# Where the last rows go: a decode step's gradient kernel, its last half of dK split in two unequal pieces, and y stored from columns

## The chip, the cores and the metric

The kernel runs on one core of one Trainium2 chip. The metric is the device time of one execution in microseconds; the span that the profile gives runs from the core's first to its last instruction and is about 2 us shorter. A core has five compute and control engines here named PE (matrix multiply), DVE (vector), ACT (scalar), POOL (GpSimd) and SP (sync), and sixteen DMA engines that move data between HBM and the on-chip memory of 128 partitions. SP, ACT and POOL each issue transfers; the transfers of one issuer form a queue (in the profile q1 is SP's, q10 is ACT's, q0 is POOL's).

## What is computed

A gated mixture of two branches for one token, forward and backward: the output y and the gradients of nine inputs.

```python
g = sigmoid((x * gate_w).sum(-1))
a = attention(x, k_cache, v_cache, wq, wo)      # 32 heads, 4096 cached keys, head size 128
b = mlp(x, w1, b1, w2)                          # 640 -> 1728 -> 640, h * tanh(softplus(h))
y = g * a + (1 - g) * b                         # out_0, [1, 1, 640], bfloat16
# and the gradients for grad_out:
# out_1 dx, out_2 dK [1, 32, 4096, 128], out_3 dV, out_4 dwq, out_5 dwo,
# out_6 dw1, out_7 db1, out_8 dw2, out_9 dgate_w [640]
```

K, V, dK and dV, 16 transfers of 2 MB each, are most of what is moved.

## The kernel before

The 32 heads are taken in 16 pairs (`i`), four pairs to a group (`g`). For a pair, K and V each come as one transfer of 2 MB: 128 partitions, 16 KB each, into one of seven buffers `kv0` to `kv6`. A pair has 16 slots; PE transposes blocks, makes the scores and the two sums, ACT copies and takes exponentials, DVE makes the outer products of dV and dK over the buffers that held V and K (`outer`, L480), and the full buffer is stored from where it lies (`store_kv`, L755). A store frees the buffer, and `pump` issues the next load. Side work of the MLP and of the projections is planned into the slots by hand.

Pair 15 is written out by hand from L892 on. Its dV and dK are made in quarters by `last_dv` and `last_dk`, and after each second quarter SP stores a half: 128 partitions of 8 KB, 1 MB. In order: the two halves of dV (L900), then the two of dK (L906); between them ACT stores two halves of dwo (L358), and POOL the last of dwq (L514, 640 rows of 1 KB).

At the very end come y, dx and the gradient of `gate_w`. Each stands as 128 partitions by 5 columns in one tile, `fin[:, 0, :]`, `fin[:, 1, :]` and `fin[:, 2, :]`: element 5p + c is in partition p, column c. `fin[:, 0, :]` (y) is written first, at L949; the others need a sum over the partitions on PE (L956) and follow at L959 and L963. PE transposes the three into rows (L967), DVE copies them to `frow`, three partitions of 640 elements (L969), and SP stores each row from one partition in one or two transfers of L976: 640; 636 and 4; 637 and 3 elements. The lengths keep each transfer in one piece on one DMA engine.

Transfers signal their end on semaphores that are taken up in turn: eight for those of SP and ACT together, eight for POOL's. Before a semaphore is used again, the issuing engine waits until the transfer that used it last has landed everywhere. At the end, L1002 in the profile, SP waits for all of these semaphores one after the other, two by two with POOL's; then all engines meet at drains and the program ends.

Of the kernel before, what the change touches and what calls it, by code (L numbers as in the profile page):

```python
# [17 lines left out]
def kernel(  # L18
# [33 lines left out]
    nc = tc.nc  # L52
    P = 128
    _, H, Sk, Dh = A_k_cache.shape
    D = A_x.shape[-1]
# [5 lines left out]
    RC = D // P  # L61
# [16 lines left out]
    dKv = out_2.rearrange("b (i h) (p j) d -> (b i) (h p) (j d)", h=2, j=J)  # L78
# [23 lines left out]
    def C(shape, dt, name):  # L102
        return const.tile(shape, dt, name=name, tag=name)
# [3 lines left out]
    bufs = [big.tile([P, bufw.get(i, KVW)], BF16, name=f"kv{i}", tag=f"kv{i}") for i in range(NBUF)]  # L107
# [369 lines left out]
    def outer(b, col, row, q):  # L477
        n = J // 4
        j0 = q * n
        nc.vector.tensor_tensor(  # L480
            kview(b)[:, j0:j0 + n, :].rearrange("p j (a b) -> p j a b", b=2),
            col[:, j0:j0 + n, :].unsqueeze(2).to_broadcast([P, n, Dh // 2, 2]),
            row.rearrange("p (a b) -> p a b", b=2).unsqueeze(1).to_broadcast([P, n, Dh // 2, 2]),
            ALU.mult)
# [215 lines left out]
    for g in range(NG - 1):  # L700
        i = 4 * g + 4
# [16 lines left out]
    for g in (2, 3):  # L718
        i = 4 * g
# [8 lines left out]
    g, i = NG - 1, NP - 2  # L728
# [163 lines left out]
    i, g = NP - 1, NG - 1  # L892
    q = i % 4
    fb = free_q.popleft()
# [7 lines left out]
    def last_dk(t):  # L902
        outer(fb, st[i]["ds"], Qr[g % 2][:, q, :], t)
        if t % 2:
            h = slice((t - 1) * KVW // 4, (t + 1) * KVW // 4)
            nc.sync.dma_start(dKv[i][:, h], bufs[fb][:, h])  # L906

    for s in range(8):
        slot(i, s)
# [23 lines left out]
    last_dv(2)  # L933
    last_dv(3)
    last_dk(0)
    last_dk(1)
    for rc in range(RC):
        dx_sum(g, NG + g, CB, GC, rc)
        dwq_row(g, CB, GC, rc)
    st_dwq(g * GC + CA, (g + 1) * GC, nc.gpsimd)  # L940
    last_dk(2)
    last_dk(3)

    fin = C([P, 3, RC], BF16, "fin")
# [2 lines left out]
    gb = C([P, RC], F32, "gb")  # L947
    nc.vector.tensor_scalar(gb[:], b_acc[:], omg[:], None, ALU.mult)
    nc.vector.tensor_tensor(fin[:, 0, :], ga[:], gb[:], ALU.add)  # L949
    amb = C([P, RC], F32, "amb")  # L950
    nc.vector.tensor_tensor(amb[:], a_acc[:], b_acc[:], ALU.subtract)
    dgp = C([P, 1], F32, "dgp")
# [14 lines left out]
        nc.tensor.transpose(fr_ps[:, c, :], fin[:, :, c], idb[:])  # L967
    frow = C([3, P, RC], BF16, "frow")
    nc.vector.tensor_copy(frow[:].rearrange("r p c -> r c p"), fr_ps[:])  # L969
    flat = frow[:].rearrange("r p c -> r (p c)")  # L970
    for r, (n, v) in enumerate(((5, out_0.rearrange("a b n -> (a b) n")), (6, out_1.rearrange("a b n -> (a b) n")),
                                (7, out_9.rearrange("(a n) -> a n", a=1)))):
        m = D // n * n
        for c0, c1, k in ((0, m, n), (m, D, 1)):
            if c1 > c0:
                nc.sync.dma_start(v[:, c0:c1].rearrange("a (n x) -> a n x", n=k),  # L976
                                  flat[r:r + 1, c0:c1].rearrange("a (n x) -> a n x", n=k))

# [1 line left out]
_INS = ['A_x', 'A_k_cache', 'A_v_cache', 'A_wq', 'A_wo', 'B_x', 'B_w1', 'B_b1', 'B_w2', 'gate_w', 'grad_out']  # L980
# [26 lines left out]
```

## Time and profile before

| | us |
|---|---|
| median of 3 runs | 404.56 (403.58 to 404.89) |
| profiled execution, its time | 404.45 |
| profiled execution, its span | 402.3 |
| DVE done with `fin[:, 0, :]` | 386.7 |
| SP's issue of the last half of dK | 386.3 |
| DVE done with `frow` | 391.6 |
| SP's issues of the small stores | 391.6 to 396.5 |

Times inside the execution are from the start of its span. The DMA engines moved 164.71 MB in 15867 packets, 409 GB/s on the mean: half of it reading HBM, half of it writing. PE, DVE and ACT are busy for 76, 73 and 66% of the span, POOL for 6%. A packet in the page's sense is one run of bytes moved by one DMA engine; a semaphore's update by a DMA engine is a packet of 4 bytes. A landing is the moment at which the update of a semaphore is recorded.

### The profile page before, as it was taken

How to read it: one execution, taken by the hardware profiler on the slowest of the kernel's cores; microseconds unless marked ns; L12 is line 12 of the kernel's file. 1: busy time of each engine (PE TensorE's matmuls, PEld its weight loads, DVE VectorE, ACT ScalarE, POOL GpSimd, SP SyncE). 2: the span in 40 equal slices, each digit the busy share in tenths (PEclk: the TensorE clock that was granted, in tenths of full speed). 3: DMA queues.
4: the chain of work that ended last, by engine and by line, in shares of the span. 5: the costliest groups of instructions: out<-in, count | busy, mean ns of one | idle time of the engine just before them, and what ended most of it. 6: DMA issues, size and time to landing. Idle time of an engine off the chain costs nothing.

```text
span 402.3 us, 10310 instructions
## 1 busy us (share of the span) xinstructions
PE 303.7 (76%) x4242; PEld 249.0 (62%) x4249; DVE 293.4 (73%) x650; ACT 264.2 (66%) x539; POOL 23.6 (6%) x47
## 2 busy tenths in 40 slices
PE   3879977987778675978889969845789898887410
PEld 3567866866567564866678748725568676675200
DVE  3759677789876595979887948751895697788770
ACT  3547453677567867787766668843377998876730
POOL 3000100001000010100001000000000000000000
PEclk9989998999899699999999989988699899999655
DMA  8999999999999999999999999999999999999992
GB/s 274 428 408 428 427 422 423 428 418 389 414 425 426 420 368 427 422 427 429 433 428 423 430 423 435 423 427 427 428 424 433 424 418 425 421 426 428 402 413 83
DMA packets 15867, 164.71 MB, mean 409 GB/s; under 512 B 1624, under 2 KB 1819, under 8 KB 6092
## 3 DMA queue, kind: packets, MB, share of 16 engines
q1 hardware_dynamic: 8842, 94.08, 55.8%
q0 software_dynamic: 5376, 63.42, 37.5%
q10 hardware_dynamic: 1602, 6.56, 4.3%
q8 instruction: 33, 0.54, 0.5%
q14 instruction: 14, 0.11, 0.1%
HBM read 82.03 MB, written 82.03 MB: 408 GB/s over the span
## 4 chain that ended last, share of the span: by engine, by line
DMA 31%; issue 20%; PE 18%; DVE 17%; ACT 9%; POOL 1%; SPq 1%; ACTq 0%; POOLq 0%; DVEq 0%
DMA wq<-in_A_wq_dram 10%; DVE kv L480 9%; PE tr L374 7%; DMA out_dram<-kv 6%; DMA wo<-in_A_wo_dram 6%; DMA wq<-in_B_w_dram 6%; DMA kv<-in_A_k_cache_dram 4%; ACT tch L377 3%; PE tr L448 2%; PE S L384 2%; DVE junk L290 1%; ACT p_dup L424 1%; PE dq L434 1%; PE a_ps L340 1%; ACT tch L443 1%
## 5 line engine op out<-in xcount | busy, mean ns | idle before, releaser
L377 ACT COPY tch<-tr 128x512 f32<-128x512 f32 x256 | 145.1, 587 | 65.3 <-PE tr L374 60.1
L374 PE MATMUL tr<-idf,kv 128*128 128x128 f32 x1024 | 171.6, 294 | 21.1 <-DMA kv<-in_A_v_cache_dram 10.5
L374 PEld LDWEIGHTS tr<-idf,kv 128*128 128x128 f32 x1024 | 119.7, 150 | 49.3 <-issue 32.4
L384 PEld LDWEIGHTS <-tch 128*128 128x128 bf16 x2048 | 89.7, 98 | 21.6 <-ACT tch L377 15.4
L480 DVE TENSOR_TENSOR kv<-p_dup,Dr 128x2048 bf16<-128x2048 bf16 x64 | 76.8, 1220 | 19.7 <-ACT p_dup L424 19.4
L480 DVE TENSOR_TENSOR kv<-ds_dup,Qr 128x2048 bf16<-128x2048 bf16 x64 | 76.8, 1220 | 0.4
L384 PE MATMUL dP<-dR,tch 128*128 128x48 bf16 x1024 | 47.1, 185 | 10.5 <-ACT tch L377 10.3
L384 PE MATMUL S<-qR,tch 128*128 128x48 bf16 x1024 | 47.7, 186 | 1.1 <-ACT tch L377 0.5
L290 DVE SCALAR_TENSOR_TENSOR junk<-wo,da_bc 128x640 bf16<-128x640 bf16 x32 | 26.3, 822 | 13.8 <-DMA wo<-in_A_wo_dram 13.1
L448 PE MATMUL tr<-idf,tch 128*128 128x128 f32 x128 | 22.0, 297 | 18.2 <-ACT tch L443 18.0
L757 POOL DMA_DIRECT2D out_dram<-kv x25 | 13.4, 536 | 297.1 <-DVE kv L480 251.9
L448 PEld LDWEIGHTS tr<-idf,tch 128*128 128x128 f32 x128 | 14.0, 145 | 20.8 <-ACT tch L443 19.8
L352 ACT ACTIVATE wq<-dqrow,xf 128x1024 bf16<-128x1024 bf16 (+2 forms) x30 | 25.1, 860 | 2.6 <-DVE wq L507 2.3
L507 DVE SCALAR_TENSOR_TENSOR wq<-wq,dqrow 128x1024 bf16<-128x1024 bf16 (+2 forms) x30 | 25.1, 863 | 0.2
L434 PE MATMUL o<-kv,e_m 128*32 128x512 bf16 x256 | 20.4, 400 | 0.0
L434 PE MATMUL dq<-kv,ds_m 128*32 128x512 bf16 x256 | 19.5, 384 | 0.9 <-DVE ds_m L470 0.9
L424 ACT ACTIVATE p_dup<-e_m,rz 64x128 bf16<-64x128 bf16 x32 | 12.7, 397 | 7.7 <-DVE rz L418 7.3
L352 ACT ACTIVATE wo<-da_bc,o8f 128x640 bf16<-128x640 bf16 x20 | 15.9, 825 | 1.3 <-PE a_ps L340 0.8
L411 ACT ACTIVATE e_m<-S,negM 64x64 bf16<-64x64 f32 x32 | 10.5, 329 | 6.3 <-DVE negM L406 5.7
L281 ACT CAST Qr<-q_ps 64x256 bf16<-64x256 f32 x16 | 5.9, 367 | 12.3 <-PE q_ps L277 12.2
L474 ACT COPY ds_dup<-ds_m 64x128 bf16<-64x128 bf16 x32 | 9.5, 296 | 6.4 <-DVE ds_m L470 5.8
L602 DVE SCALAR_TENSOR_TENSOR junk<-wq,db_bc 128x640 bf16<-128x640 bf16 (+1 forms) x14 | 11.5, 820 | 1.9 <-ACT db_bc L256 1.7
(169 smaller groups left out, 279.2 us busy)
## 6 DMA issues: line engine op xcount, KB each, us to landing
out_dram<-kv POOLq DMA_DIRECT2D x25, 2048.0 KB, 16.7
kv<-in_A_v_cache_dram SPq DMA_DIRECT2D x16, 2048.0 KB, 24.0
kv<-in_A_k_cache_dram SPq DMA_DIRECT2D x15, 2048.0 KB, 20.3
out_dram<-kv SPq DMA_DIRECT2D x5, 2048.0 KB, 29.3
wo<-in_A_wo_dram SPq DMA_DIRECT2D x4, 1280.0 KB, 42.9
out_dram<-kv SPq DMA_DIRECT2D x4, 1024.0 KB, 15.5
out_dram<-wo POOLq DMA_DIRECT2D x3, 1280.0 KB, 23.5
wq<-in_A_wq_dram SPq DMA_DIRECT2D x2, 1280.0 KB
```

The costliest lines, as they stand in the source:

```text
L290: nc.vector.scalar_tensor_tensor(junk[:], in0=wob[g % 2][:, k, :], scalar=1.0, in1=da_bc[:], op0=ALU.mult, op1=ALU.mult, accum_out=do8[g % ...
L352: nc.scalar.mul(dst, src, col)
L374: nc.tensor.transpose(tp[:, t, :], src[:, 4 * c + t, :], idf[:])
L377: nc.scalar.copy(dst[:].rearrange("p a b e -> p (a b e)").bitcast(F32), tp[:].rearrange("p a b -> p (a b)"))
L384: nc.tensor.matmul(ps[:, 4 * B:4 * B + W].rearrange("p (a b) -> p a b", b=4), lhsT=src[:, t, :, e], rhs=col[:, e, :, :].rearrange("p a b - ...
L424: nc.scalar.activation(p[HS[hh]], e_m[i % 2][HS[hh], 0:J, hh].unsqueeze(2).to_broadcast([64, J, 2]), ACT.Copy, scale=st[i]["rz"][HS[hh], h ...
L434: nc.tensor.matmul(st[i][key][c:c + 32].rearrange("p a b -> p (a b)"), lhsT=cols[:, 4 * g:4 * g + 16, :].rearrange("p a b -> p (a b)"), rh ...
L448: nc.tensor.transpose(tp[:, 126 * t:126 * t + P], st[i][key + "r"][:, t, :], idf[:])
L480: nc.vector.tensor_tensor(kview(b)[:, j0:j0 + n, :].rearrange("p j (a b) -> p j a b", b=2), col[:, j0:j0 + n, :].unsqueeze(2).to_broadcast ...
L507: nc.vector.scalar_tensor_tensor(w, in0=w, scalar=1.0, in1=dqrow[g % 2][:, c0:c1], op0=ALU.mult, op1=ALU.mult, accum_out=dq_acc[:, rc, par ...
L602: nc.vector.scalar_tensor_tensor(junk[0:n, :], in0=w2row(k), scalar=1.0, in1=db_bc[0:n, :], op0=ALU.mult, op1=ALU.mult, accum_out=dact[0:n ...
L757: eng.dma_start(dst, bufs[b][:, 0:J * Dh])
```

## The change

The last half of dK is stored in two transfers: first partitions 76 to 127 (52 rows), then partitions 0 to 75 (76 rows). 52 is thirteen times four, 76 is four times nineteen; the pieces are meant to run over thirteen DMA engines and over the first four. y is stored by SP directly from `fin[:, 0, :]`, five elements of 2 bytes from each partition, in four transfers of 5, 6, 7 and 110 partitions, placed in the program right after L949. The other two rows still go by way of `frow`, now in one transfer each, issued by POOL; these are cut into sixteen pieces of 40 elements in the built program. The transposes and the copy to `frow` stay as they were, the y row among them.

```diff
@@ last_dk
         if t % 2:
             h = slice((t - 1) * KVW // 4, (t + 1) * KVW // 4)
-            nc.sync.dma_start(dKv[i][:, h], bufs[fb][:, h])
+            for p0, p1 in (((76, P), (0, 76)) if t == 3 else ((0, P),)):
+                nc.sync.dma_start(dKv[i][p0:p1, h], bufs[fb][p0:p1, h])
...
     nc.vector.tensor_tensor(fin[:, 0, :], ga[:], gb[:], ALU.add)
+    y_v = out_0.rearrange("a b (p c) -> (a b p) c", c=RC)
+    for p0, p1 in ((0, 5), (5, 11), (11, 18), (18, P)):
+        nc.sync.dma_start(y_v[p0:p1], fin[p0:p1, 0, :])
...
     nc.vector.tensor_copy(frow[:].rearrange("r p c -> r c p"), fr_ps[:])
-    flat = frow[:].rearrange("r p c -> r (p c)")
-    for r, (n, v) in enumerate(((5, out_0.rearrange("a b n -> (a b) n")), (6, out_1.rearrange("a b n -> (a b) n")),
-                                (7, out_9.rearrange("(a n) -> a n", a=1)))):
-        m = D // n * n
-        for c0, c1, k in ((0, m, n), (m, D, 1)):
-            if c1 > c0:
-                nc.sync.dma_start(v[:, c0:c1].rearrange("a (n x) -> a n x", n=k),
-                                  flat[r:r + 1, c0:c1].rearrange("a (n x) -> a n x", n=k))
+    for r, v in ((1, out_1.rearrange("a b n -> (a b) n")), (2, out_9.rearrange("(a n) -> a n", a=1))):
+        nc.gpsimd.dma_start(v, frow[r:r + 1].rearrange("r p c -> r (p c)"))
```

In SP's order the second piece of the half takes a semaphore of its own, so each small store that follows uses the semaphore after the one that it had.

## The prediction

> **What bounds the kernel now.** I read the page's slices first, then busy time by stretches at the end, then the transfers inside the last stretches, and last what SP waits for. On the page DMA stands at nine tenths in nearly every slice and drops only in the last one: the kernel is bound by its transfers, and the end is theirs too. The stretches of the end (columns: us, busy time of PE, PEld, DVE, ACT and POOL with counts, granted clock, DMA share, GB/s):
>
> ```profile
> 390.00:392.00 2.00, 0.00 (x0) 0.00 (x0) 1.55 (x1) 0.00 (x0) 0.00 (x0) 0.50 1.01 417
> 392.00:394.00 2.00, 0.00 (x0) 0.00 (x0) 0.00 (x0) 0.00 (x0) 0.00 (x0) 0.50 0.87 340
> 394.00:396.00 2.00, 0.00 (x0) 0.00 (x0) 0.00 (x0) 0.00 (x0) 0.00 (x0) 0.50 0.15 59
> 396.00:398.00 2.00, 0.00 (x0) 0.00 (x0) 0.00 (x0) 0.00 (x0) 0.00 (x0) 0.50 0.06 25
> 398.00:400.00 2.00, 0.00 (x0) 0.00 (x0) 0.00 (x0) 0.00 (x0) 0.00 (x0) 0.50 0.07 29
> ```
>
> The compute engines are done at 391.6. From 396 on, 0.06 of sixteen DMA engines are busy: one engine works alone at some 26 GB/s. How the other fifteen end is in finer stretches:
>
> ```profile
> 393.20:393.60 0.40, 0.00 (x0) 0.00 (x0) 0.00 (x0) 0.00 (x0) 0.00 (x0) 0.50 0.93 362
> 393.60:394.00 0.40, 0.00 (x0) 0.00 (x0) 0.00 (x0) 0.00 (x0) 0.00 (x0) 0.50 0.47 188
> 394.00:394.40 0.40, 0.00 (x0) 0.00 (x0) 0.00 (x0) 0.00 (x0) 0.00 (x0) 0.50 0.38 154
> 394.40:394.60 0.20, 0.00 (x0) 0.00 (x0) 0.00 (x0) 0.00 (x0) 0.00 (x0) 0.50 0.21 82
> 394.60:395.90 1.30, 0.00 (x0) 0.00 (x0) 0.00 (x0) 0.00 (x0) 0.00 (x0) 0.50 0.06 25
> ```
>
> A share times 16 is the number of engines busy: 15, then 7.5, 6 and 3.4, and 1 after 394.6. So fifteen engines end between 393.5 and 394.6, on average at 393.9 (their busy time after 393.2, 10.7 us, over 15). The sixteenth, the laggard, ends at 400.54. What it moves last, between 398.08 and 400.54, and in the 2.14 us before:
>
> ```profile
> DMA packets 9, 0.07 MB, mean 27 GB/s; under 512 B 1, under 2 KB 1, under 8 KB 1
> ...
> DMA packets 11, 0.05 MB, mean 24 GB/s; under 512 B 4, under 2 KB 5, under 8 KB 5
> ```
>
> The first line is eight rows of 8 KB and one 4-byte semaphore write: the laggard's share, 8 of 128 rows, of the second half of dK (L906, issued at 386.28). Eight rows take 2.45 us, **0.306 us a row**. Before them come the rows of the first half, whose semaphore write is at 398.08. SP then waits for exactly this landing:
>
> ```profile
> SPq L1002 <- DMA out_dram<-kv: 4.4, 1, 4.4
> ...
> SPq L976 <- DMA out_dram<-kv: 2.7, 1, 2.7
> ```
>
> The semaphore events put the landings on the laggard at 391.29 and 395.93 (two halves of dV), 398.51 and 400.95 (two halves of dK). SP passes 0.02 us after the last and walks through eight more waits, 0.06 us each, to the drains; the span ends at 402.29, so 1.34 us after the landing. If the last landing is one that SP asks for five waits later, only 1.01 us follow.
>
> **The change, part by part.** *dK's last half.* One transfer of 8 rows on each of 16 engines becomes 52 rows over thirteen engines (4 each) and 76 rows over the first four (19 each). In rows: engines 13 to 15 lose 8, engines 4 to 12 lose 4, engines 0 to 3 have 23 in place of 8, so 15 more. At 0.306 us: -2.45, -1.22 and +4.59 us. No row of this trace shows a transfer split over 13 or 4 engines; the price of a row on a busy engine is bounded by the laggard's 0.306 alone and by 0.309 for the time of one packet, which is the same. The second issue costs SP another 0.33 us (the row of L906's issues) at 386.6, hidden by backlog: the fifteen other engines land the first half of dK only between 387.7 and 390.5. It uses a semaphore whose last transfer landed at 381.47, so it waits for nothing.
>
> Engines 0 to 3 now end at 393.5 to 394.6 plus 4.59: 398.1 to 399.2. Of fifteen ends that average 393.9 the latest of four lies near 394.4, so I take 399.0. The laggard ends at 398.09 if it is one of the last three, at 399.32 if it is one of the nine in the middle.
>
> *y in columns.* Four transfers of 5, 6, 7 and 110 rows of 10 bytes read fin, which DVE has at 386.72, in place of the transposed row at 391.56. SP takes up semaphores in turn, and each next use waits for the transfer that used it before: by the order of the changed program the piece of 5 waits for the store of dK of the step before (laggard, 387.22), the piece of 6 for the first half of dV (391.29), the piece of 7 for the second (395.93), the 110 go out right behind, at about 396.5. Behind SP's stall stand only these and the end. So y is not earlier, but it is in time: the small stores before took 1.06 us from issue to landing (396.21 to 397.28), which would be 397.6. On the first four engines, though, the 110 rows stand behind the 76; they land after these, at about 399.05 + 0.41 (the laggard's last row took 0.41 us from its end to its landing) = 399.45. Their packets cost little: the first loads move eight 10-byte rows in 0.015 us. This transfer is the one that SP asks for five waits later. The five old stores on SP (4.88 us from first to last, 2.7 of it the wait shown) go; they landed by 397.28 and were worth nothing.
>
> *dx and dgw on POOL.* Two stores of sixteen 80-byte pieces are issued after 391.56; POOL's issues took 0.54 us (L757) to 0.82 us (L514), so both are out by 393.3. On the laggard they stand behind POOL's last store, which ends there at 395.94, and land near 396.5. POOL's drain ended 1.69 us after its last landing (396.38 to 398.07), so now at about 398.2: cover of over a microsecond. Without that cover each microsecond would be one of time. DVE and PE get no new wait.
>
> **The sum.** The two groups race. If the laggard is one of the last three, the end is that of the first four: 399.45 + 1.01 = 400.46, so 1.83 us less. If it is one of the nine: 399.32 + 0.41 = 399.73, and 1.01 to 1.34 on top: 400.74 to 401.07, so 1.2 to 1.55 less. The profiled execution took 404.45 with a span of 402.29; it stands 0.11 under the median of 404.56. From that median: 402.7, or 403.0 to 403.35. What I forecast is **402.8**, the first case leaning to the second. The ends of the first case are 398.1 and 399.2 for the first four, so 399.56 to 400.66 of span, 401.8 to 402.9.
>
> The Trainium skill ("DMA: Bandwidth & Descriptors", section "Latency and other measured facts") calls DMA engines 7 and 15 the usual slow ones. No run here names the laggard's number; 15 would give the 402.7 above and 7 the 403.0.
>
> **The rivals.** *The laggard is among the first four: slower.* Then its last half costs 15 rows more, +4.59 us, less the 0.33 for the order of waits: 404.56 + 4.26 = 408.8. It decides from the place of one engine. For it: any engine but one is possible. Against: the 1280-byte stores of L976 are each one packet on one engine, and that engine had its rows done by 394, so at least one of the low places is not the laggard's. By counting the fifteen left, 3 in 15; I give 0.13, as the next rival takes some too.
>
> *The first four become the bound altogether.* It is the same price of 4.59 us against the laggard's lead, 400.54 - 394.6 = 5.9 us at least. The change pays only while that lead exceeds 4.6 less the 0.33. Here it does by 1.7 us; an execution with a lead of 4 us would be 0.3 us slower. The semaphore events show the lead as it grows: 0.3 to 0.5 us around 140, 4.2 at 299, 6.5 at 376, 6.6 at the end; steady at the end, and the three times lie within 1.3 us. This is inside the forecast's spread, with 0.05 on the slower side.
>
> The Trainium skill (same page, section "Rules for kernel authors") speaks against such splits: two transfers to disjoint partitions share the same engines, so one transfer of 128 partitions is better. That holds for engines that end together; the rows above show one that ends 6 us late. With even ends it would make the last half 4.59 us dearer.
>
> *The split does not fall as it says.* If both pieces spread evenly over all sixteen engines, the laggard keeps about 8 rows and lands at 400.95; what is left is the 0 to 0.33 us of the order of waits: 404.2 to 404.6. For it: no transfer of 13 or 4 engines is in this trace. Against: a row of 1280 bytes did go to one engine alone. I give 0.10.
>
> **How the numbers follow.** Forecast case 0.77, laggard in the first four 0.13, no split 0.10. About 0.3% (1.2 us) is what a measurement of this kernel can tell from no change. In the forecast case the gain is 1.2 to 1.85 us with a spread of half a microsecond between executions: 0.58 faster, 0.14 within, 0.05 slower. The split rival gives 0.02 faster, 0.07 within, 0.01 slower; the laggard rival 0.13 slower. Together 0.60, 0.21, 0.19. The range runs from 401.6 (ends of the first four at their earliest, and 0.2 of noise) to 404.6 (no split), and leaves out the laggard rival and 0.05 of tails.
>
> **What would show it.** In the changed profile: after about 394.6 four or five engines are busy (a share of 0.25 to 0.3) until near 398, with the rate at 100 to 130 GB/s; the last landing near 399.5, and the span near 400.5. A share of 0.06 to the end with a span over 402 means that nothing moved; one engine alone to past 404 means that the laggard is one of the four. POOL's drain past 399 would mean that dx and dgw have become the end. A piece of 110 that is issued after 397 breaks the reading of SP's waits.

## The result, and the profile after

| | before | after |
|---|---|---|
| median, same chip and session | 404.37 (403.05 to 406.31) | 406.61 (404.43 to 408.62) |
| ratio | | 1.0053, interval 1.0037 to 1.0070 |
| profiled execution, its time | 404.45 | 408.19 |
| profiled execution, its span | 402.3 | 406.0 |

The kernel became slower, by 2.2 us; 1.8 us less had been forecast, and 406.61 lies above the range. The profiled execution stands 1.6 above its own median: it issues the last half of dK at 387.90, against 386.28 before. That lag arose near 200 us, far ahead of anything the change touches (the 57th of the 128 outer products of `outer` began at 202.9, against 200.5), and another execution of the same program, experiment e1, had that one at 199.9. So 1.6 us of what follows is taken off as drift.

The stretches of the end, of the changed kernel, with the columns of the prediction's first fence (the 16 DMA engines' share and GB/s last):

```profile
394.00:396.00 2.00, 0.00 (x0) 0.00 (x0) 0.00 (x0) 0.00 (x0) 0.52 (x2) 0.50 0.55 206
396.00:398.00 2.00, 0.00 (x0) 0.00 (x0) 0.00 (x0) 0.00 (x0) 0.00 (x0) 0.50 0.36 138
398.00:400.00 2.00, 0.00 (x0) 0.00 (x0) 0.00 (x0) 0.00 (x0) 0.00 (x0) 0.50 0.37 78
400.00:402.00 2.00, 0.00 (x0) 0.00 (x0) 0.00 (x0) 0.00 (x0) 0.00 (x0) 0.50 0.22 82
402.00:404.00 2.00, 0.00 (x0) 0.00 (x0) 0.00 (x0) 0.00 (x0) 0.00 (x0) 0.50 0.04 13
```

The split does what it says: after 396 five engines and more are busy (0.36 times 16), not one. But between 398 and 400 the same share moves 78 GB/s in place of 138: the engines are occupied and deliver little. What the changed kernel moved from 397.3 to 398.9, and from 398.9 to 400.5:

```profile
DMA packets 105, 0.21 MB, mean 131 GB/s; under 512 B 79, under 2 KB 79, under 8 KB 80
...
DMA packets 15, 0.07 MB, mean 46 GB/s; under 512 B 6, under 2 KB 6, under 8 KB 6
```

79 packets in the first stretch are small: 60 of them are ten-byte pieces of y, all between 397.5 and 398.2. They are gone by 398.9, and in the 1.6 us behind them only nine rows get through. Single rows of 8 KB took up to 1.57 us here, where the price was 0.306. SP's waits for landings of stores from `kv`, at the end and at the store of y:

```profile
SPq L1000 <- DMA out_dram<-kv: 3.4, 2, 2.6
SPq L953 <- DMA out_dram<-kv: 3.4, 2, 3.0
```

By the semaphore events the 76 rows land at 402.42, 402.73, 402.79 and 404.29, the last 1.5 us after the last row's end (402.82). Then the four pieces of y land one behind the other, at 404.47, 404.64, 404.82 and 405.00. SP passes its last waits 0.17 to 0.18 us apart in place of 0.06, and is done at 405.2.

### The profile page after: what moved, and what is told of

It is laid out like the page before. It is cut to its first block, busy times and chain, and to the rows that moved or that the text cites. A ratio compares the mean times of both kernels' runs of the same rounds, so it can differ in the third digit from the quotient of the medians.

```text
span 406.0 us, 10320 instructions
## 1 busy us (share of the span) xinstructions
PE 309.6 (76%) x4249; PEld 252.6 (62%) x4249; DVE 293.5 (72%) x650; ACT 264.1 (65%) x539; POOL 24.6 (6%) x49
## 4 chain that ended last, share of the span: by engine, by line
issue 28%; DMA 26%; DVE 17%; PE 14%; ACT 9%; POOL 1%; SPq 1%; POOLq 0%; ACTq 0%; DVEq 0%
DMA out_dram<-kv 11%; DVE kv L480 9%; DMA wo<-in_A_wo_dram 6%; DMA kv<-in_A_k_cache_dram 6%; PE tr L374 5%; DMA kv<-in_A_v_cache_dram 4%; ACT tch L377 3%; DVE junk L290 3%; PE tr L448 2%; PE S L384 1%; PE a_ps L340 1%; ACT tch L443 1%; PE dq L434 1%; ACT p_dup L424 1%; DVE wq L507 1%
## 5 line engine op out<-in xcount | busy, mean ns | idle before, releaser
L374 PE MATMUL tr<-idf,kv 128*128 128x128 f32 x1024 | 173.4, 296 | 18.4 <-DMA kv<-in_A_k_cache_dram 9.5
L374 PEld LDWEIGHTS tr<-idf,kv 128*128 128x128 f32 x1024 | 121.5, 152 | 46.9 <-issue 31.9
L384 PEld LDWEIGHTS <-tch 128*128 128x128 bf16 x2048 | 91.0, 99 | 22.6 <-ACT tch L377 16.1
L384 PE MATMUL S<-qR,tch 128*128 128x48 bf16 x1024 | 48.7, 188 | 1.1 <-ACT tch L377 0.5
```

The costliest lines, as they stand in the source:

```text
L374: nc.tensor.transpose(tp[:, t, :], src[:, 4 * c + t, :], idf[:])
L384: nc.tensor.matmul(ps[:, 4 * B:4 * B + W].rearrange("p (a b) -> p a b", b=4), lhsT=src[:, t, :, e], rhs=col[:, e, :, :].rearrange("p a b - ...
```

## The experiments

Each kernel ran beside the kernel before on the same chip. Theory A puts the loss on the split: rows piled on four engines cost more there than the laggard's price. Theory B puts it on y's ten-byte stores. Runs e1 to e4, e5 to e8 and e9 to e11 are one session each (before: 404.52, 404.68 and 404.89), each session on another chip.

**The changed kernel again (e1), no edit.**

> The changed kernel unaltered, for a second profile and for times beside those of the runs that follow. Theory A (the pile): the 19 rows on each of the first four engines set the end, and they cost more than the 0.306 us a row of the prediction, because engines that end together hold each other up, as five of them did from 398.9 to 400.5 in the profile after (46 GB/s where 131 went before). Theory B (the small stores): the 10-byte stores behind the rows land one after the other, 0.17 us each, and POOL's two stores hold its drain to 404.5; the rows alone would be a gain of 1.2 to 1.8 us, as forecast. Theory C (one execution): the stall is chance and the profiled one was unlucky. Expected by A and B: 406.0 to 407.0 median, 1.6 to 2.4 us over the kernel before, the last landing of the 76 rows at 402.5 or later; by A the rate in the last 5 us before the last row falls under 100 GB/s again; by C there is no such fall, and the span is under 404.5.

405.53, ratio 1.0020 [1.0003, 1.0037]: slower again, by 1.0 us, and 1.1 under the first session's median; 406.0 to 407.0 had been expected. The two intervals just touch at their ends: the change costs 2.2 us in one session and 1.0 in the other. Times below are compared with the kernel before in the same session. Its end, in stretches:

```profile
397.10:398.10 1.00, 0.00 (x0) 0.00 (x0) 0.00 (x0) 0.00 (x0) 0.00 (x0) 0.50 0.35 132
398.10:399.10 1.00, 0.00 (x0) 0.00 (x0) 0.00 (x0) 0.00 (x0) 0.00 (x0) 0.50 0.14 42
399.10:401.40 2.30, 0.00 (x0) 0.00 (x0) 0.00 (x0) 0.00 (x0) 0.00 (x0) 0.50 0.00 0
```

Here the rows end at 398.93 and the last packet at 399.04. That is as early as the prediction had it, but only because this execution issues the half at 385.32, 1.0 us earlier than before. Then nothing moves for 2.3 us: the share is 0.00. The landings of dK come until 401.43, the last ones of y's four pieces from 401.62 to 402.18. The fall of the rate that theory A asked for isn't there, and the span of 403.2 is under the 404.5 of theory C (a chance stall in the first profile); but the time is lost here too. In one execution it goes in long packets, in the other between the last packet and its landing; a price per packet sees neither.

**The split alone (e2).** Old small stores, dK in two pieces:

```diff
-            nc.sync.dma_start(dKv[i][:, h], bufs[fb][:, h])
+            for p0, p1 in (((76, P), (0, 76)) if t == 3 else ((0, P),)):
+                nc.sync.dma_start(dKv[i][p0:p1, h], bufs[fb][p0:p1, h])
```

> The kernel before with the last half of dK as 52 and 76 rows; the small stores as before, from rows, by SP. Theory A (the pile): slower than before by 1.3 to 2.3 us, with the four engines ending at 401 or later by the profile. Theory B (the small stores): faster than before by 1 to 1.8 us, the last landing near 399.5 to 400, as the prediction had it.

404.14, ratio 0.9991 [0.9977, 1.0005]: neither figure. The split alone does not slow the kernel, so A's loss of 1.3 to 2.3 us isn't there; the full gain of B does not come either. Its end in stretches, and its longest wait at the end:

```profile
394.60:396.60 2.00, 0.00 (x0) 0.00 (x0) 0.00 (x0) 0.00 (x0) 0.00 (x0) 0.50 0.31 125
396.60:398.60 2.00, 0.00 (x0) 0.00 (x0) 0.00 (x0) 0.00 (x0) 0.00 (x0) 0.50 0.31 127
398.60:400.60 2.00, 0.00 (x0) 0.00 (x0) 0.00 (x0) 0.00 (x0) 0.00 (x0) 0.50 0.14 59
```
```profile
SPq L1003 <- DMA out_dram<-kv: 1.3, 2, 0.9
```

Five engines at a share of 0.31 and 125 GB/s: this is the picture the prediction drew, and the rows follow one another at 0.306 us on each. On the first four engines they end at 399.34, 399.45, 399.88 and 399.93. The 76 rows land at 400.27 at the latest, the 52 on the laggard at 399.82. But the last of the five small stores is issued only at 398.6 and stands on the first engine behind the pile; SP's last waits then go from 400.28 to 401.17, 0.89 us where five of 0.06 had been. Some 0.6 us of the gain is spent there.

Another part is lost ahead of all this. In the kernel before, the stretch from 390 to 392 has a share of 1.01 and 417 GB/s (the first line of the prediction's first fence). The same stretch here (first line) and in e9 (second line), which has the same split and no column store either:

```profile
390.00:392.00 2.00, 0.00 (x0) 0.00 (x0) 1.56 (x1) 0.00 (x0) 0.00 (x0) 0.50 0.98 263
390.00:392.00 2.00, 0.04 (x1) 0.00 (x0) 1.91 (x1) 0.00 (x0) 0.00 (x0) 0.50 0.96 230
```

The engines are nearly as occupied as before and deliver 63 and 55% of it. 19 of the 31 rows begun in this stretch of e2 took more than 0.35 us, the longest 1.20; before, none of 82 did. All seven kernels with the last half in two pieces show it (230 to 330 GB/s), and none of the six with the half in one (380 to 427). From 388 to 394 the rows of e2 took 10.9 us more than at 0.309 each, some 0.7 us for each of sixteen engines if it falls on them evenly (an estimate). So rows are also stretched without any ten-byte write, by the split itself; what in it does so, no run separates.

**The small stores alone (e3).** The changed kernel with dK whole:

```diff
-            for p0, p1 in (((76, P), (0, 76)) if t == 3 else ((0, P),)):
-                nc.sync.dma_start(dKv[i][p0:p1, h], bufs[fb][p0:p1, h])
+            nc.sync.dma_start(dKv[i][:, h], bufs[fb][:, h])
```

> The kernel before with the last half of dK whole, and y stored from columns by SP in pieces of 5, 6, 7 and 110, dx and the gradient of gate_w by POOL, as in the changed kernel. Theory A (the pile): within 0.6 us of before, up to 0.7 slower from the small stores' landings in a row behind the laggard's last rows. Theory B (the small stores): slower by 1.5 us or more, with POOL's drain or the 110 rows of y as the last to end.

406.37, ratio 1.0043 [1.0028, 1.0058]: 1.85 us slower with no split at all. Its stretches around the piece of 110 partitions, then its transfers from 398.23 to 400.315 and from 400.325 to 402.49:

```profile
397.20:398.20 1.00, 0.00 (x0) 0.00 (x0) 0.00 (x0) 0.00 (x0) 0.00 (x0) 0.50 0.11 26
398.20:400.30 2.10, 0.00 (x0) 0.00 (x0) 0.00 (x0) 0.00 (x0) 0.00 (x0) 0.50 0.06 12
400.30:402.40 2.10, 0.00 (x0) 0.00 (x0) 0.00 (x0) 0.00 (x0) 0.00 (x0) 0.50 0.07 27
```
```profile
DMA packets 6, 0.02 MB, mean 12 GB/s; under 512 B 3, under 2 KB 3, under 8 KB 3
...
DMA packets 9, 0.07 MB, mean 30 GB/s; under 512 B 1, under 2 KB 1, under 8 KB 1
```

Of the rows, only the laggard's are left, and most of the loss can be read off this one engine: from 398.2 to 400.3 its rate is 12 GB/s, before and after 26 and 27. Three rows took 0.65, 0.63 and 0.80 us in place of 0.31, 1.14 us lost; the next eight went at 0.306 again. That is where 100 of the 110 ten-byte writes, whose packets ran from 397.2 to 397.6, land on ten other engines (397.97 to 399.77). At the end the landings follow one another from 403.21 to 403.96, and from the first of them to the end of the span it is 1.83 us, 0.48 more than before. Together that makes 1.6 of the 1.85 us. All four pieces of y land late on the laggard, the piece of five too, so the laggard is one of the first five engines.

**A pile on the first four, nothing else (e4).** 4 and 124 rows; 124 is four times 31, so all 128 rows go to the first four, 32 each:

```diff
-            nc.sync.dma_start(dKv[i][:, h], bufs[fb][:, h])
+            for p0, p1 in (((124, P), (0, 124)) if t == 3 else ((0, P),)):
+                nc.sync.dma_start(dKv[i][p0:p1, h], bufs[fb][p0:p1, h])
```

> The kernel before with the last half of dK as 4 and 124 rows, both of a number of rows that puts them on the first four engines: 32 rows on each of the four, none on the other twelve; small stores as before. It measures the price of a row on the four: against 52 and 76 rows (23 on each of the four) nine rows more. Prediction's price (0.306 us a row, no collisions): the four end 24 rows, 7.3 us, later than in the kernel before, at about 401.7, so 1.2 us slower than before and 2.8 slower than the kernel with 52 and 76 rows alone. Theory A (the pile costs more than that): 4 to 6 us slower than before. Theory B says the same as the prediction's price.

406.70, ratio 1.0075 [1.0046, 1.0103], 2.2 us slower by the medians, where 1.2 had been expected by the price; three of the twelve times lie at 410.4 to 410.9 and lift the ratio. Its end in stretches:

```profile
396.00:398.00 2.00, 0.00 (x0) 0.00 (x0) 0.00 (x0) 0.00 (x0) 0.00 (x0) 0.50 0.31 131
...
398.40:400.00 1.60, 0.00 (x0) 0.00 (x0) 0.00 (x0) 0.00 (x0) 0.00 (x0) 0.50 0.24 102
400.00:401.80 1.80, 0.00 (x0) 0.00 (x0) 0.00 (x0) 0.00 (x0) 0.00 (x0) 0.50 0.25 102
```

Five engines until 398.12, when the laggard ends by itself; then four, at 102 GB/s, 25 each. Nothing is dear about the pile once only four engines are left: rows that follow one another begin 0.306 us apart here too. Against e2 each of the four has nine rows more, and the latest ends at 402.88 against 399.93, 2.95 us; by the price it would be 2.75. The laggard is not among the first four; with e3 it is the fifth. The miss over the 1.2 us is the base: 402.88 less 24 rows (32 less the 8 they had before) of 0.306 is 395.5, not 394.4.

**y in columns, alone (e5).** dK whole; dx and dgw as rows by SP, one transfer each:

```diff
+    for p0, p1 in ((0, 5), (5, 11), (11, 18), (18, P)):
+        nc.sync.dma_start(y_v[p0:p1], fin[p0:p1, 0, :])
...
-    for r, (n, v) in enumerate(((5, out_0...), (6, out_1...), (7, out_9...))):
+    for r, n, v in ((1, 5, out_1...), (2, 5, out_9...)):
```

> The kernel before with y alone stored from columns by SP (5, 6, 7 and 110 partitions, ten bytes each, right after L949); the last half of dK whole; dx and the gradient of gate_w by SP from rows, one transfer each. Theory B1 (ten-byte writes): the hundred-odd ten-byte writes take 1 to 2.5 us to land, and rows that other engines write meanwhile, the laggard's among them, take 0.6 to 0.8 us in place of 0.31; with four landings in a row behind the laggard's last (0.18 us each in place of 0.06) that makes 1.2 to 1.9 us over the kernel before. Theory B2 (POOL): the two stores that moved to POOL are the cost, by what they put on the laggard's queue and by POOL's drain; y from columns then costs under 0.5 us.

406.25, ratio 1.0041 [1.0023, 1.0059]: the loss of e3 without POOL's part. Transfers in its windows 394.91 to 396.75, 396.75 to 398.45 and 398.44 to 400.28:

```profile
DMA packets 119, 0.05 MB, mean 28 GB/s; under 512 B 112, under 2 KB 113, under 8 KB 113
...
DMA packets 4, 0.02 MB, mean 14 GB/s; under 512 B 1, under 2 KB 1, under 8 KB 1
...
DMA packets 9, 0.06 MB, mean 32 GB/s; under 512 B 1, under 2 KB 2, under 8 KB 2
```

112 small packets go by in the first window with the laggard at its usual rate. In the second, behind them, it gets three packets over 8 KB through in 1.7 us: two rows took 0.635 and 1.056 us, 1.07 lost. In the third window it is back at the usual rate. The same print as in e3, at another time and on one engine alone. The profiled execution is the fastest of eight (404.98): it issues the half at 385.21, 1.07 us earlier than before, which in this one execution makes up for the rows.

**dx and dgw on POOL, alone (e6).** dK whole, y as a row by SP:

```diff
-    for r, (n, v) in enumerate(((5, out_0...), (6, out_1...), (7, out_9...))):
+    for r, n, v in ((0, 5, out_0...),):
...
+    for r, v in ((1, out_1...), (2, out_9...)):
+        nc.gpsimd.dma_start(v, frow[r:r + 1].rearrange("r p c -> r (p c)"))
```

> The kernel before with dx and the gradient of gate_w alone on POOL (sixteen pieces of 80 bytes each); y by SP from its row as before, the last half of dK whole. Theory B1 (ten-byte writes): within 0.5 us of before, POOL's drain ending over a microsecond ahead of SP. Theory B2 (POOL): slower by 1.2 us or more.

404.50, ratio 0.9990 [0.9972, 1.0008]: nothing. Thirty-two pieces of 80 bytes, stored by POOL, hold up no row. With e5 the parts add up roughly: +1.6 and -0.2, against +1.85 in e3, which is of another session.

**y eight microseconds earlier (e7).** `fin[:, 0, :]` is made right behind the sum it needs and stored in one transfer of 128 partitions at 380.70, when all engines are still loaded:

```diff
     a_cols(g)
+    ...
+    nc.vector.tensor_tensor(fin[:, 0, :], ga[:], gb[:], ALU.add)
+    y_v = out_0.rearrange("a b (p c) -> (a b p) c", c=RC)
+    nc.sync.dma_start(y_v, fin[:, 0, :])
```

> The kernel before with y made right after a_acc, some 8 us earlier than before, and stored at once from columns by SP in one transfer of 128 partitions; dx and the gradient of gate_w by SP from rows, one transfer each. Nothing of y is left behind the last rows. Theory B1 in its strong form (ten-byte writes hold up all rows wherever they fall): slower than before by 0.8 to 1.5 us, since the laggard is busy then too. In its weak form (only what stands on the path at the end costs): within 0.5 us of before. Theory B2: within 0.5 us.

405.42, ratio 1.0029 [1.0010, 1.0047]: 0.7 us by the medians, between the two bands expected, and not free there either. Its stretches around most of the ten-byte packets (381.5 to 382.4):

```profile
381.50:382.50 1.00, 0.00 (x0) 0.00 (x0) 1.00 (x2) 1.00 (x2) 0.00 (x0) 0.50 0.49 173
382.50:383.50 1.00, 0.00 (x0) 0.00 (x0) 1.00 (x2) 0.55 (x2) 0.00 (x0) 0.50 0.35 57
383.50:384.50 1.00, 0.00 (x0) 0.00 (x0) 1.00 (x2) 1.00 (x2) 0.00 (x0) 0.50 0.91 329
```

57 GB/s at a share of 0.35, and three of the five rows begun in that microsecond took 1.01 to 1.33 us. But a share of 0.35 also says that engines lacked queued work, and three small operations of DVE (0.55 us) came forward with y. How the 0.7 us divides between these is open; only the long rows are the print of e3 and e5.

**60 and 68 rows, the three rows by POOL (e8).** 60 is fifteen times four, 68 four times seventeen; y joins dx and dgw on POOL:

```diff
-            for p0, p1 in (((76, P), (0, 76)) if t == 3 else ((0, P),)):
+            for p0, p1 in (((68, P), (0, 68)) if t == 3 else ((0, P),)):
...
-    for p0, p1 in ((0, 5), (5, 11), (11, 18), (18, P)):
-        nc.sync.dma_start(y_v[p0:p1], fin[p0:p1, 0, :])
...
-    for r, v in ((1, out_1...), (2, out_9...)):
+    for r, v in ((0, out_0...), (1, out_1...), (2, out_9...)):
```

> A candidate for a better version: the last half of dK as 60 rows (fifteen engines, 4 each) and 68 (the first four, 17 each), and y, dx and the gradient of gate_w all from rows by POOL, so that SP has nothing behind the rows. Against the kernel with 52 and 76 rows alone (0.4 us faster than before) the first four have two rows less (0.6 us) and the landings behind them, 0.9 us in that profile, shrink to the waits' 0.3. Theory B1: 0.8 to 1.5 us faster than before. Theory B2: no faster than before, as POOL's three stores and its drain end last.

405.45, ratio 1.0022 [1.0004, 1.0041]: a miss. The drains at its end:

```profile
L998 POOLq DRAIN  x3: 40/93/8694, 393.7 to 402.9; - x3
L998 SPq DRAIN  x3: 7/7/7, 401.7 to 402.7; - x3
```

POOL's first drain starts at 393.7 and takes 8.69 us, to 402.4; SP stands ready at 401.7. So POOL sets the end, by 0.7 us. Its pieces on the first four engines wait among their many rows, the last lands at 400.61, and the drain ends 1.8 us after that.

**The changed kernel with y as a row (e9).** The split and POOL's stores of dx and dgw stay; only y goes back to one transfer from `frow`, by SP:

```diff
-    for p0, p1 in ((0, 5), (5, 11), (11, 18), (18, P)):
-        nc.sync.dma_start(y_v[p0:p1], fin[p0:p1, 0, :])
...
+    nc.sync.dma_start(out_0..., flat[0:1]...)
```

> The changed kernel with one part undone: y goes by SP from its row, in one transfer on one engine, as before the change; the 52 and 76 rows and POOL's two stores stay. Theory B1 (ten-byte writes are the cost): 1.2 to 2.2 us faster than the changed kernel, so 0 to 1 us faster than before, like the kernel with the split alone. If the split and the rest were the cost (theory A): within 0.5 us of the changed kernel, 1 us or more slower than before.

403.50, ratio 0.9963 [0.9949, 0.9978]: 1.4 us faster than before, more than the 0 to 1 expected. The one edit against the changed kernel turns the sign. Its end in stretches:

```profile
395.60:396.60 1.00, 0.00 (x0) 0.00 (x0) 0.00 (x0) 0.00 (x0) 0.00 (x0) 0.50 0.31 127
...
397.60:398.60 1.00, 0.00 (x0) 0.00 (x0) 0.00 (x0) 0.00 (x0) 0.00 (x0) 0.50 0.32 131
398.60:399.60 1.00, 0.00 (x0) 0.00 (x0) 0.00 (x0) 0.00 (x0) 0.00 (x0) 0.50 0.29 123
399.60:400.60 1.00, 0.00 (x0) 0.00 (x0) 0.00 (x0) 0.00 (x0) 0.00 (x0) 0.50 0.04 18
```

Five engines at 123 to 131 GB/s with no gap up to 399.6: the stretch that broke down to 78 in the changed kernel is whole. The first four end between 399.24 and 400.39, the 76 rows land at 400.71, 0.3 us behind, and SP is done at 401.16. POOL's drain ends at 401.1, level with it.

**Two rows in columns (e10).** dK whole; y and dx each in two transfers of 18 and 110 partitions:

```diff
+    for p0, p1 in ((0, 18), (18, P)):
+        nc.sync.dma_start(y_v[p0:p1], fin[p0:p1, 0, :])
...
+    for p0, p1 in ((18, P), (0, 18)):
+        nc.sync.dma_start(x1_v[p0:p1], fin[p0:p1, 1, :])
```

> The kernel before with two outputs from columns in place of one: y in pieces of 18 and 110 partitions, and dx likewise, all by SP; the gradient of gate_w from its row; the last half of dK whole. The dose is doubled: 256 ten-byte writes in place of 128. Theory B1: each hundred or so of these writes costs the laggard about 1.1 us in slowed rows, twice 1.1, and landings in a row behind its last rows up to 0.4: 2 to 3 us slower than before, against 1.6 with y alone from columns. If it is the number of landings at the end and not the writes (theory B3): 1.6 us or less, as with y alone.

407.08, ratio 1.0051 [1.0032, 1.0071], 2.2 us: in the band expected if ten-byte writes hold rows up. In its trace four rows begun between 394.2 and 396.5 took 0.60 to 0.94 us, 1.7 us more than at 0.309, against 1.07 in e5. But the interval overlaps that of e5 (one column store, 1.0041), so that a second one adds its full price is not shown.

**60 and 68 rows, the three rows by ACT (e11).** e8 with the three rows from ACT, one transfer each in one piece:

```diff
-        nc.gpsimd.dma_start(v, frow[r:r + 1].rearrange("r p c -> r (p c)"))
+        nc.scalar.dma_start(v..., flat[r:r + 1]...)
```

> A second candidate: the last half of dK as 60 rows (fifteen engines) and 68 (the first four), and y, dx and the gradient of gate_w from rows, one transfer each, issued by ACT, whose queue on the first engine does not stand behind SP's rows. No ten-byte write, nothing of SP's behind the rows, no drain of POOL behind late landings (it held the kernel with POOL's three stores for 0.7 us). By B1 and by the rows: the end is the later of the first four (two rows less than with 52 and 76) and the laggard (four rows less than before): 0.5 to 1.2 us faster than before.

403.89, ratio 0.9973 [0.9959, 0.9987]: 1.0 us faster. Against e8 the ratio is lower by 0.5%; the profiles put 0.7 us of that on POOL's drain. e9 has the lowest time of all, and its interval overlaps this one.

## Why the prediction was wrong, point by point

**Right: the bound, how the split falls, and the price of a row at the end.** The laggard sits in the middle nine (the fifth engine), gives up four rows and ends with the others; five engines stay busy; with only these left, a row costs 0.306 us on any of them. With y as a row (e9) the gain is 1.4 us, inside the 1.2 to 1.85 of the forecast case. That is in part luck: e9's own profile, less the 0.44 us by which it issues the half later, has a span only 0.75 us shorter than before, because the first four end later than was priced (below). None of the three rivals came about: the laggard is not among the first four (e4), the first four end last but do not cost the whole gain (e9), and the split falls as it says.

**Wrong, and the step that turned the sign: "Their packets cost little: the first loads move eight 10-byte rows in 0.015 us".** That priced ten-byte *writes to HBM* by the packet time of *loads*, and those loads stand in the trace as one packet of 80 bytes each (0.015 us), not eight of ten. What the writes do to rows of other engines was put at nothing. Their packets are short too, 0.007 to 0.009 us each; what is long is the time until they have landed and what it does to others. In e3 and e5, with no split, rows on the laggard lose 1.14 and 1.07 us while the writes land on other engines. In the changed kernel the 22 rows begun between 398.7 and 401.3 took 6.05 us more than at 0.309 each, 1.2 us for each of the five engines at work. The landing 0.41 us after the rows, of the sentence before, failed too: 1.5 us in the profile after, 2.5 in e1, 0.3 in e9, which has no such writes.

**Wrong in sign: "1.01 us follow" in place of 1.34.** Putting y's piece five waits later was counted as 0.33 us of gain. The four pieces of y land one after another, and from the last row's landing to the end of the span the profile after has 1.7 us.

**Mis-sized: the base of the first four, 394.4.** It came from the mean of fifteen ends. Taking the added rows at 0.306 off the end of the rows gives 395.3 in e2, whose issue of the half is at 386.28 as before, and 395.5 and 395.8 in e4 and e9, which issue it 0.3 and 0.4 us later: about 0.9 us more in each. The prediction held the price of a row on a busy engine to 0.306 and 0.309, from a kernel with the half in one piece. The rows that the split stretches between 390 and 392, up to 1.2 us each, are what the traces have in its place; that they make up the whole 0.9 is not shown.

**Wrong, without effect on the end: POOL's drain "at about 398.2".** The prediction looked at the laggard alone. POOL's pieces also stand among the rows of the first four: their last landing is at 402.71, the drain ends at 404.48, and SP is later only because of y. In e9 the cover is under 0.1 us, in e8 it is gone.

With the terms put right, the sum nearly closes. Predicted end of span 400.46; drift 1.6; base 0.9; rows held up while the writes land 1.2, as measured above (these three make 3.7, and the rows end at 402.82 in place of 399.0, 3.8 later); landing 1.5 in place of 0.45, 1.0; after the landing 1.7 in place of 1.0, 0.7. Together 405.9, measured 406.0. The base comes from other executions, so an agreement this close is in part chance.

**Left open.** y in columns costs 1.6 us alone (e5); from the changed kernel to e9, in other sessions, it is 1.0 or 2.2 plus 1.4, so 2.4 to 3.6. Why it should cost more with the split, and how much of that is between sessions, no run separates. Nor does any run show what in the hardware holds the rows. With the half in one piece they are long while ten-byte writes land, on an engine that has none of these writes to move at the time; with it in two they are long near 391 without such writes as well. Whether the ten bytes, the number of pieces or the neighbouring addresses they write make y's stores costly isn't separated either: e6 has pieces of 80 bytes, fewer of them, and from POOL.

## What to carry to other kernels

Price a store by its landing and by what other engines' packets do meanwhile, not by its packets' own time; in this kernel a row of 640 elements is better written from one partition in one piece than from 128 in pieces of ten bytes. Work may be taken off a lagging engine at the row price, so long as everything else that stands on the newly loaded engines, small stores and the pieces of a queue that is drained at the end, is counted with it. When a change bundles several edits, sum and test them apart: here the split with y as a row was worth -1.4 us (e9) and y in columns alone +1.6 (e5). And look at the rates ahead of the end as well: two pieces in place of one cost something 8 us before it.

## What the runs showed of the hardware

- Ten-byte writes to HBM (y's piece of 110 partitions, on eleven engines) have packets of 0.007 to 0.009 us and land 0.4 to 2.5 us later (e3, e5, the changed kernel); 8-KB writes of other engines take from 0.63 to 1.06 us (e3, e5) and up to 1.57 (the changed kernel) in that time, in place of 0.31. The Trainium skill ("DMA: Bandwidth & Descriptors", section "Specifications") says that below 512 bytes the engine does a read-modify-write; the long landings could be that, but no trace shows it, and that 80-byte pieces cost nothing (e6) shows that being under 512 bytes alone doesn't decide.
- With the last half stored in two pieces, all engines together moved 230 to 330 GB/s between 390 and 392 us (the changed kernel, e1, e2, e4, e8, e9, e11), against 380 to 427 with it in one (before, e3, e5, e6, e7, e10); single 8-KB rows took up to 1.2 us there.
- Small stores that stand behind a loaded engine land in a row, 0.17 to 0.19 us apart (e1, e2, e3, the changed kernel), where SP's waits for landed ones take 0.06.
- SP's issue of the 76 rows, right behind that of the 52 (0.39 us), took 1.07 us in the changed kernel, against 0.33 for 128 partitions before. In e4 the 4 rows took 0.33 and the 124 behind them 1.07, so it isn't the four engines alone; whether it is the number of rows on them or the issue just ahead is not separated.
- POOL's drain ended 1.7 to 1.8 us after POOL's last landing in three kernels (before, the changed one, e8).
- The lagging engine is the fifth, by which transfers reach it (e3, e4; both of one chip). The Trainium skill (same page, section "Latency and other measured facts") calls 7 and 15 the usual slow ones; counted in this order, neither was the one that set the end on this chip.
